# Retention and gated experts on one core: norm steps on VectorE, operand sums one chunk later, other order of the products

## The chip, the cores and the metric

The kernel runs on one core of one Trainium2 chip. A core has five engines with queues of their own: TensorE (PE in the rows; PEld is its weight load), VectorE (DVE), ScalarE (ACT), GpSimd (POOL) and SyncE (SP, which here issues most DMAs), and 16 DMA engines. The metric is the device time of one execution in microseconds (us).

## The reference

Three steps, one after the other: a retention (linear attention with a decay per head), an RMS norm with a SiLU-gated block, and four ReLU experts weighted by normalised probabilities.

```python
# B=2, H=8, S=768, D=64; gamma = 1 - 2**(-5-h), scale = 1/8
for t in range(S):
    state = gamma * state + einsum('bhd,bhe->bhde', k[:, :, t], v[:, :, t])
    y[:, :, t] = scale * einsum('bhd,bhde->bhe', q[:, :, t], state)
x = y.transpose(0, 2, 1, 3).reshape(1536, 512)
xn = x / sqrt(mean(x * x, -1) + 1e-6) * rms_g
g = xn @ w_gate                                  # 512 x 1536
x2 = (g * sigmoid(g) * (xn @ w_val)) @ w_out     # 1536 x 512
p = probs / (probs.sum(-1, keepdims=True) + 1e-9)
out = sum(p[:, e:e+1] * (relu(x2 @ w1[e]) @ w2[e]) for e in range(4))
```

## The kernel before

**Retention.** The 768 tokens of each of the two batches are cut into six chunks of 128, which makes twelve chunks in a row (i = 0 to 11; the profile's f32 matmuls of 64 to 128 columns). Inside a chunk the decay is a mask on the scores; between chunks a state per head pair is carried. For chunk i the steps are: `load` (two DMAs of up to 512 KB on SP's queue: `qk`, and `vk`, which is v and a second layout of k), `prep` (k times its decay `gk`, on GpSimd), `scores` (16 records, L727, into two PSUM banks), `masked` (L734: scores times `mask` into `am`, two VectorE products), `q_table` (L711, a matmul that spreads five small tables `gq` over partitions, copied by ACT), `prep_q` (L704: q times `gq`, on GpSimd or VectorE), `mix` (L745: `am` times v, 8 matmuls of 64 columns; L755: the state's copy `S` times q, 4 matmuls of 128 columns, added to them; then on ACT square with a row sum L765, root L767 and `vv` L769; then the state's update L781 and ACT's two copies of it, L789). A matmul of f32 shows as two records in the rows, so a chunk has 16 records of L745 and 8 of L755.

**Norm and operands.** `normal` takes the reciprocal of the root (L796, VectorE) and refines it by one Newton step in three ACT instructions (L799 to L801), with `vv`, `less` and `more` as its inputs; `normal2` (L807, VectorE) multiplies row and gain and writes `xn`. `to_x` turns `xn` by four transposes into a PSUM bank (L829) and makes from it operands of a block product in which 7 products do the work of 8. Each operand is kept as two fp32r halves, hi and lo. A chunk of a batch's first block (chunks 0 to 2 and 6 to 8) is split from the bank (hi on ACT, L839; lo on VectorE, L842) and copied for later (`first`, L845). A chunk of the second block needs sums with `first`: B22's hi (L857, ACT), two sums (L859, L861) and B22's lo (L863), all of the last three on VectorE, then two more sums and the splits of `tsum` (`split`, L815 and L818).

**Order.** In iteration i of the chunk loop TensorE does scores(i+1), mix(i), the state of i and the transposes of chunk i−1. Between the steps `pace.fill` lets waiting tasks in: conversion and sums of weights, splits, weight loads. `Pace` keeps an estimated clock for each queue (`work`, `did`, `need`), and a task goes to the engine that it reckons free first; where a task has a choice (`"PV"`), the estimate decides between GpSimd and VectorE. The order on each engine is fixed when the program is built. Buffers rotate: three for each load, two for `am`, `xn` and `tsum`, one for `first`, six PSUM banks.

**Start.** Ten zero matmuls (`warm`, L718) fill TensorE, then two matmuls (L913) spread the decays from two small inputs, `right` and `left`, then two more zeros, scores(0) and scores(1). DMAs that SP and ACT issue use eight semaphores in turn; the ninth issue waits for the landing of the first, and so on.

**After the retention** come the products of the gate, value and output matrices and of the experts (`winograd`, L523; `kept` L532 holds partial results), up to the end at 850 us.

## Time and profile before

| what | value |
| --- | --- |
| time, median of 3 (lowest to highest) | 851.85 us (851.7 to 852.69) |
| profiled execution | 851.76 us |
| its span in the trace | 850.0 us |
| TensorE busy | 835.3 us, 98% |
| VectorE, ScalarE, GpSimd busy | 543.8, 433.3, 582.0 us |
| chain that ended last | PE 86%, DVE 6%, ACT 4% |

The span is what the trace covers; the 1.76 us to the profiled execution's time lie around it. Times in the rows count from the span's start. A busy share is a mean over stages, so the stages are looked at one by one in the rows below: the stretch up to 9.3 us is the start, up to about 75 us the retention runs with weight conversion beside it, and from there on the products.

### The profile page before, as it was taken

The numbers are of one execution on the slowest core, as the hardware profiler recorded it, in microseconds if no ns is written. First come the engines' busy times: TensorE is split into PE (matmuls) and PEld (weight loads), VectorE is DVE, ScalarE is ACT, GpSimd is POOL, SyncE is SP. The second block draws the span as 40 slices with busy tenths as digits, with TensorE's granted clock in tenths as the row PEclk, the third lists the DMA queues.
The fourth block names the chain that finished last, engine by engine and source line by source line (L and its number), as shares of the span: only waits on it lengthen the run. The fifth ranks groups of instructions, "written<-read, shape, count | busy, mean of one in ns | idle before, by whom it ended". The sixth has DMA issues, their size and how long they took to land.

```text
span 850.0 us, 13945 instructions
## 1 busy us (share of the span) xinstructions
PE 835.3 (98%) x5167; PEld 795.3 (94%) x5167; DVE 543.8 (64%) x976; ACT 433.3 (51%) x971; POOL 582.0 (68%) x710
## 2 busy tenths in 40 slices
PE   8989999999999999899999999999999999999998
PEld 7879999999999999889999999999999999999987
DVE  4886867779686847842665565566466466556664
ACT  4788765445443546566444534544545454454421
POOL 3456847364454558669789888988988988988500
PEclk9999999999999999999999999999999999999999
DMA  8941232212122101100110111011011011101003
GB/s 274 308 167 51 75 100 75 75 59 91 51 74 76 49 25 27 38 25 25 50 38 27 37 38 38 26 43 33 25 51 27 25 50 38 34 30 38 1 13 136
DMA packets 29232, 52.37 MB, mean 62 GB/s; under 512 B 3988, under 2 KB 12724, under 8 KB 29164
## 3 DMA queue, kind: packets, MB, share of 16 engines
q1 hardware_dynamic: 28880, 51.24, 19.0%
q8 instruction: 40, 0.66, 0.3%
q10 hardware_dynamic: 284, 0.24, 0.1%
q14 instruction: 28, 0.23, 0.1%
HBM read 48.33 MB, written 3.15 MB: 61 GB/s over the span
## 4 chain that ended last, share of the span: by engine, by line
PE 86%; DVE 6%; ACT 4%; POOL 1%; issue 1%; DMA 1%; SPq 0%; DVEq 0%; ACTq 0%
PE bank L523 42%; PE bank L1231 7%; PE bank L1269 6%; PE bank L1270 6%; PE bank L1268 6%; PE cross L1231 5%; PE bank L1082 3%; PE bank L1083 3%; PE bank L1081 3%; PE bank L745 2%; DVE s L616 1%; POOL x2Tlo L1034 1%; PE bank L727 1%; DMA qk<-in_qk_dram 1%; DVE kept L613 1%
## 5 line engine op out<-in xcount | busy, mean ns | idle before, releaser
L532 ACT COPY kept<-bank 128x384 f32<-128x384 f32 x168 | 80.7, 481 | 122.2 <-PE bank L523 111.8
L1208 DVE SCALAR_TENSOR_TENSOR oacc<-cross,p_sb,oacc 128x256 f32<-128x256 f32 (+1 forms) x126 | 65.6, 566 | 64.2 <-PE cross L1231 64.2
L1276 DVE SCALAR_TENSOR_TENSOR oacc<-bank,p_sb,oacc 128x512 f32<-128x512 f32 (+1 forms) x97 | 72.2, 745 | 51.9 <-PE bank L1270 51.8
L1137 POOL TENSOR_TENSOR hs<-h,hs 128x384 fp32r<-128x384 f32 x97 | 97.7, 1023 | 0.7 <-ACT hs L1135 0.6
L523 PE MATMUL bank<-x2Thi,widehi 128*128 128x384 f32 x256 | 87.8, 343 | 0.7 <-DVE kept L1114 0.7
L523 PE MATMUL bank<-x2Thi,widelo 128*128 128x384 f32 x256 | 86.1, 336 | 0.0
L523 PE MATMUL bank<-x2Tlo,widehi 128*128 128x384 f32 x256 | 85.9, 336 | 0.0
L1270 PE MATMUL bank<-plainhi,hs 128*128 128x512 f32 (+1 forms) x218 | 85.1, 390 | 0.0
L1269 PE MATMUL bank<-plainlo,hs 128*128 128x512 f32 (+1 forms) x218 | 85.0, 390 | 0.0
L1268 PE MATMUL bank<-plainhi,hs 128*128 128x512 f32 (+1 forms) x218 | 84.3, 387 | 0.0
L621 POOL TENSOR_TENSOR hlo<-s,hhi 128x384 fp32r<-128x384 f32 x48 | 52.9, 1104 | 30.7 <-ACT hhi L618 24.1
L1117 ACT ACTIVATE hs<-kept 128x384 fp32r<-128x384 f32 x54 | 28.5, 527 | 86.9 <-DVE kept L1114 86.8
L1082 PE MATMUL bank<-hlo,plainhi 128*128 128x384 f32 x192 | 64.4, 335 | 1.8 <-POOL hlo L621 1.8
L523 PE MATMUL bank<-xThi,widehi 128*128 128x384 f32 x192 | 64.4, 336 | 0.0
L523 PE MATMUL bank<-xThi,widelo 128*128 128x384 f32 x192 | 64.2, 334 | 0.0
L523 PE MATMUL bank<-xTlo,widehi 128*128 128x384 f32 x192 | 64.2, 334 | 0.0
L1083 PE MATMUL bank<-hhi,plainlo 128*128 128x384 f32 x192 | 64.1, 334 | 0.0
L1081 PE MATMUL bank<-hhi,plainhi 128*128 128x384 f32 x192 | 64.1, 334 | 0.0
L1208 DVE SCALAR_TENSOR_TENSOR oacc<-bank,p_sb,oacc 128x512 f32<-128x512 f32 x84 | 59.2, 745 | 6.4 <-PE bank L1231 6.4
L464 POOL TENSOR_TENSOR downlo<-down,downhi 128x512 fp32r<-128x512 f32 x28 | 36.3, 1299 | 37.3 <-ACT downhi L460 37.3
L395 POOL TENSOR_TENSOR widelo<-sums,widehi 128x512 fp32r<-128x512 f32 x44 | 58.0, 1317 | 5.3 <-ACT widehi L390 4.9
L1143 POOL TENSOR_TENSOR h<-h 128x384 f32<-128x384 f32 x55 | 56.0, 1018 | 4.2 <-ACT h L1156 2.2
(182 smaller groups left out, 2538.8 us busy)
## 6 DMA issues: line engine op xcount, KB each, us to landing
wst<-in_moe_w_dram SPq DMA_DIRECT2D x64, 256.0 KB, 2.8
qk<-in_qk_dram SPq DMA_DIRECT2D x12, 512.0 KB, 5.7
wst<-in_moe_w_gate_dram SPq DMA_DIRECT2D x12, 512.0 KB, 3.8
wst<-in_moe_w_val_dram SPq DMA_DIRECT2D x12, 512.0 KB, 3.8
wst<-in_moe_w_out_dram SPq DMA_DIRECT2D x12, 512.0 KB, 3.8
vk<-in_vk_dram SPq DMA_DIRECT2D x10, 512.0 KB, 5.7
out_dram<-oacc SPq DMA_DIRECT2D x11, 256.0 KB, 2.0
vk<-in_vk_dram SPq DMA_DIRECT2D x2, 256.0 KB, 4.4
```

Source lines behind the costliest of these rows:

```text
L523: nc.tensor.matmul(out=ps, lhsT=lhs, rhs=rhs, start=(first and j == i == 0), stop=(j == KH - 1 and i == 2), skip_group_check=not first,)
L532: nc.scalar.copy(out=t, in_=ps)
L1081: nc.tensor.matmul(out=ps, lhsT=whi[:, c], rhs=hi, start=(f == 0), stop=False)
L1082: nc.tensor.matmul(out=ps, lhsT=whi[:, c], rhs=lo, start=False, stop=False)
L1083: nc.tensor.matmul(out=ps, lhsT=wlo[:, c], rhs=hi, start=False, stop=(f == NF - 1))
L1137: 0, "PV", TB, lambda eng: eng.tensor_tensor(out=lo, in0=t, in1=hi.bitcast(F32), op=ALU.subtract), [high]
L1208: run = lambda eng: eng.scalar_tensor_tensor(out=acc, in0=ps, scalar=pe, in1=acc, op0=ALU.mult, op1=ALU.add)
L1231: nc.tensor.matmul(out=where[c], lhsT=lhs[:, cols], rhs=rhs, start=bool(i == 0 and opens and opens(c)), stop=(i == 2), skip_group_check=True,)
L1268: nc.tensor.matmul(out=ps, lhsT=hi[:, c], rhs=whi[:, cols], start=(f == 0), stop=False)
L1269: nc.tensor.matmul(out=ps, lhsT=hi[:, c], rhs=wlo[:, cols], start=False, stop=False)
L1270: nc.tensor.matmul(out=ps, lhsT=lo[:, c], rhs=whi[:, cols], start=False, stop=(f == NF - 1))
L1276: nc.vector.scalar_tensor_tensor(out=acc, in0=ps, scalar=pe, in1=acc, op0=ALU.mult, op1=ALU.add)
```

## The change

1. **Norm's steps.** The ACT instruction for `vv` and the three of the Newton step become one `tensor_scalar` and two `scalar_tensor_tensor` on VectorE around the reciprocal (four VectorE instructions of 128x1 per chunk). `less` and `more` are gone.
2. **Operand sums later.** `to_x` is cut in two: the transposes stay, and what reads their bank (`from_x`) is kept in `taken_x` for chunks 1 to 9 and issued in the next iteration behind `normal2`.
3. **First block.** ACT copies the bank to `first`; hi and lo are split from that copy, lo on GpSimd or VectorE.
4. **Start.** `right` is loaded on SP's queue, ahead of all; seven zeros stand between scores(0) and scores(1); q_table(0) and q_table(1) come after the products of chunk 0, and q of chunk 1 is multiplied then.
5. **Products alternate.** In chunks with a state each product with `S` is issued right behind the first of its two products with `am`, so `q task` and `S end` are needed ahead of all.
6. **The planner's numbers.** A load counts 440 instead of 390 per half and 2.0 more for `vk`; a pair of products counts 0.68 (0.46 without a state).

```diff
-            end = pace.work("D", n * 390, pace.now)
+            end = pace.work("D", n * 440, pace.now) + (2.0 if nm == "vk" else 0.0)
...
+            if c:
+                pace.matmuls(0, pace.need(st[i]["q task"]), st[i]["S end"])
             for n in range(NP):
                 for j in range(2):
                     nc.tensor.matmul(
                         out=y[:, 2 * n + j, :], lhsT=am[:, j, n, :], rhs=vt[:, 2 * n + j, :],
...
-                pace.matmuls(0.4)
+                    if c and j == 0:
+                        nc.tensor.matmul(
+                            out=y[:, 2 * n:2 * n + 2, :].rearrange("p h d -> p (h d)"), lhsT=pairs(st[i]["q"])[:, n, :],
+                            rhs=st[i]["S"][:, n, :], start=False, stop=True, skip_group_check=True,
+                        )
+                pace.matmuls(0.68 if c else 0.46)
...
+            if i == 0:
+                q_table(0)
+                prep_q(1)
...
-            nc.scalar.activation(out=vv, in_=ss, func=AF.Identity, scale=-0.5 / DM, bias=less)
...
+            nc.vector.tensor_scalar(
+                out=vv, in0=ss, scalar1=-0.5 / DM, scalar2=-0.5 * EPS, op0=ALU.mult, op1=ALU.add
+            )
             nc.vector.reciprocal(out=r1, in_=r0)
-            end = pace.did("V", 1, end)
-
-            nc.scalar.activation(out=r0, in_=r1, func=AF.Square)
-            nc.scalar.activation(out=r2, in_=r0, func=AF.Identity, scale=vv, bias=more)
-            nc.scalar.activation(out=r1, in_=r1, func=AF.Copy, scale=r2)
-            end = pace.work("A", 420, end)
+            nc.vector.scalar_tensor_tensor(out=r2, in0=r1, scalar=r1, in1=vv, op0=ALU.mult, op1=ALU.mult)
+            nc.vector.scalar_tensor_tensor(out=r1, in0=r2, scalar=1.5, in1=r1, op0=ALU.add, op1=ALU.mult)
+            end = pace.did("V", 450, end)
...
             st[i].clear()
+            if 0 < i < NS - 2:
+                taken_x.append(lambda: from_x(i, ps))
+            else:
+                from_x(i, ps)
...
-                high = pace.add(1, "A", DM, lambda eng: eng.copy(out=hi, in_=ps), [pace.done(pace.now)])
-
-                low = pace.add(
-                    1, "V", DM, lambda eng: eng.tensor_tensor(out=lo, in0=ps, in1=hi.bitcast(F32), op=ALU.subtract),
-                    [high], port=False,
-                )
                 nc.scalar.copy(out=b1, in_=ps)
-                pace.did("A", DM)
...
+                split(b, first_block[b, "readers"], [pace.done(pace.did("A", DM))], hi, lo, b1, DM)
...
-        nc.scalar.dma_start(out=right, in_=c_right)
+        nc.sync.dma_start(out=right, in_=c_right)
...
+            if i == 0:
+                warm(7)
             if i + 1 < NS:
                 scores(i + 1)
-                for x in ((0, 1), (2, 3), (4,))[i] if i < 3 else ():
+                for x in ((), (2, 3), (4,))[i] if i < 3 else ():
                     q_table(x)
-                prep_q(i + 1)
+                if i:
+                    prep_q(i + 1)
                 masked(i + 1)
             if 0 < i < NS - 1:
                 normal2(i - 1)
+            while taken_x:
+                taken_x.pop()()
...
             mix(i)
+            if i == 0:
+                q_table(1)
```

TensorE's queue, from the program's start to the state of chunk 0 (`zeros` are warm, `rights,lefts` the decays, `qk` scores, `q_rows,picks` a q_table, `vk,am` products, `state` the state), before:

```order
L718 MATMUL bank<-zeros 128x128 x10
L913 MATMUL bank<-rights,lefts 128x512 x2
L718 MATMUL bank<-zeros 128x128 x2
L727 MATMUL bank<-qk 128x128 x16
L711 MATMUL bank<-q_rows,picks 128x512 x2
L745 MATMUL bank<-vk,am 128x64 x8
L781 MATMUL state<-vk 64x64 x8
```

and now:

```order
L910 MATMUL bank<-rights,lefts 128x512 x2
L718 MATMUL bank<-zeros 128x128 x2
L727 MATMUL bank<-qk 128x128 x8
L718 MATMUL bank<-zeros 128x128 x7
L727 MATMUL bank<-qk 128x128 x8
L747 MATMUL bank<-vk,am 128x64 x8
L711 MATMUL bank<-q_rows,picks 128x512
L780 MATMUL state<-vk 64x64 x8
L711 MATMUL bank<-q_rows,picks 128x512
```

The two scores stand seven zeros apart, and the two tables have moved behind the products and behind the state.

SP's queue at the start, with the semaphores of earlier DMAs (DMAHW) that an issue waits for, before:

```order
L678 DMA qk<-in_qk_dram 128x1024
L885 DMA square<-in_c_square_dram 128x128
L678 DMA vk<-in_vk_dram 128x1024
L896 DMA gk<-in_c_k_dram 128x48
L678 DMA qk<-in_qk_dram 128x1024
L678 DMA vk<-in_vk_dram 128x1024 [waits DMAHW2_49]
```

and now (DMAHW0 is `right`'s, DMAHW1 `left`'s, DMAHW2 that of the first `qk`):

```order
L879 DMA right<-in_c_right_dram 16x1024
L678 DMA qk<-in_qk_dram 128x1024
L882 DMA square<-in_c_square_dram 128x128
L678 DMA vk<-in_vk_dram 128x1024
L893 DMA gk<-in_c_k_dram 128x48 [waits DMAHW0_49]
L678 DMA qk<-in_qk_dram 128x1024 [waits DMAHW1_49]
L678 DMA vk<-in_vk_dram 128x1024 [waits DMAHW2_49]
```

`right` is issued first, and `gk` and the second `qk`, which waited for nothing, wait for a landing each.

VectorE's queue around the first chunk with sums (`r` are the norm's small steps, `am` the masked scores), before:

```order
L859 TENSOR_TENSOR tsum<-bank,first 128x256
L861 TENSOR_TENSOR tsum<-bank,tsum 128x256
L863 TENSOR_TENSOR xB22lo_89<-bank,xB22hi_88 128x2x128
L796 RECIPROCAL r_526<-r_525 128x1
L734 TENSOR_TENSOR am<-bank,mask 128x512 x2
L807 SCALAR_TENSOR_TENSOR xn<-bank,r_526,g_sb 128x512
```

and now:

```order
L795 TENSOR_SCALAR vv<-ss 128x1
L798 RECIPROCAL r_525<-r_524 128x1
L799 SCALAR_TENSOR_TENSOR r_526<-r_525,vv 128x1
L800 SCALAR_TENSOR_TENSOR r_525<-r_526,r_525 128x1
L734 TENSOR_TENSOR am<-bank,mask 128x512 x2
L806 SCALAR_TENSOR_TENSOR xn<-bank,r_525,g_sb 128x512
L857 TENSOR_TENSOR tsum<-bank,first 128x256
L859 TENSOR_TENSOR tsum<-bank,tsum 128x256
L861 TENSOR_TENSOR xB22lo_89<-bank,xB22hi_88 128x2x128
```

The three instructions that read the bank of the transposes stand behind the next `xn` instead of ahead of the norm, and the norm's other small steps stand with the reciprocal.

## Rows read from the trace of the kernel before

**Rows 1.** Busy us (instructions) of PE, PEld, DVE, ACT, POOL; clock, DMA share, GB/s

```profile
9.30:34.30 25.00, 25.00 (x275) 22.05 (x277) 17.77 (x35) 19.13 (x53) 10.41 (x9) 1.00 0.91 300
34.30:68.42 34.12, 30.79 (x356) 27.59 (x357) 27.91 (x58) 26.06 (x79) 19.23 (x20) 1.00 0.51 180
...
100.00:300.00 200.00, 199.68 (x1147) 198.23 (x1146) 148.50 (x280) 104.33 (x229) 103.32 (x129) 1.00 0.23 72
```

**Rows 2.** Timeline of TensorE, start: start us, us, instruction [idle before <- releaser]

```profile
1.05 4.63 PE L718 MATMUL bank<-zeros 128*128 128x128 f32 x20 [1.05 <-DVE zeros L890]
6.47 0.83 PE L913 MATMUL bank<-rights,lefts 128*128 128x512 f32 x2 [0.79 <-DVE lefts L909]
7.14 0.60 PE L718 MATMUL bank<-zeros 128*128 128x128 f32 x4
7.68 1.16 PE L727 MATMUL bank<-qk 64*128 64x128 f32 x16
9.30 1.16 PE L727 MATMUL bank<-qk 64*128 64x128 f32 x16 [0.46 <-DMA qk<-in_qk_dram]
```

**Rows 3.** DMA issues of 1 to 3.5 us: KB, median us to landing

```profile
qk<-in_qk_dram SPq DMA_DIRECT2D x2, 512.0 KB, 6.5
...
right<-in_c_right_dram ACTq DMA_DIRECT2D x1, 64.0 KB, 4.6
```

**Rows 4.** Timeline of the queues' DMA issues at the start

```profile
0.87 0.40 ACTq L882 DMA_DIRECT2D right<-in_c_right_dram  x1
...
2.78 0.44 SPq L678 DMA_DIRECT2D qk<-in_qk_dram  x1
```

**Rows 5.** DMA issues of the stretch 18.3 to 19 us, the same columns

```profile
qk<-in_qk_dram SPq DMA_DIRECT2D x1, 512.0 KB, 3.9
```

**Rows 6.** Waits of TensorE, 34.3 to 68.42 us: total, times, longest us

```profile
PE bank L829 <- DVE xn L807: 2.7, 4, 1.3
PE bank L727 <- DMA qk<-in_qk_dram: 0.7, 1, 0.7
```

**Rows 7.** Timeline of all queues, 34 to 42 us

```profile
34.31 0.33 SPq L315 DMA_DIRECT2D wst<-in_moe_w_out_dram  x1
...
34.73 0.38 SPq L678 DMA_DIRECT2D qk<-in_qk_dram  x1
...
41.07 1.16 PE L727 MATMUL bank<-qk 64*128 64x128 f32 x16 [0.66 <-DMA qk<-in_qk_dram]
```

**Rows 8.** Chain of waits, one chunk: start us, us, what

```profile
25.13 1.09 PE bank L727 x16
26.22 1.93 PE bank L745 x16
28.15 0.95 PE bank L755 x8
...
29.71 0.59 PE bank L829 x4
```

**Rows 9.** Timeline of VectorE and ScalarE, 36 to 40 us

```profile
36.57 0.42 DVE L859 TENSOR_TENSOR tsum<-bank,first 128x256 f32<-128x256 f32 x1 [0.83 <-ACT xB22hi L857]
...
37.70 0.15 DVE L796 RECIPROCAL r<-r 128x1 f32<-128x1 f32 x1
...
38.61 0.30 ACT L801 ACTIVATE r<-r,r 128x1 f32<-128x1 f32 x1
...
38.96 0.74 DVE L807 SCALAR_TENSOR_TENSOR xn<-bank,r,g_sb 128x512 f32<-128x512 f32 x1
```

**Rows 10.** Timeline of ScalarE and TensorE, 45 to 49 us

```profile
46.24 0.73 ACT L789 COPY S<-state 64x256 f32<-64x256 f32 x2
...
46.73 2.00 PE L745 MATMUL bank<-vk,am 128*128 128x64 f32 x16
```

**Rows 11.** Instructions by line and form, L704: ns min/median/max, starts

```profile
L704 DVE TENSOR_TENSOR qk<-qk,gq x2: 685/988/1292, 51.4 to 55.6; 128x512 f32<-128x512 f32 x2
```

**Rows 12.** Timeline of TensorE, 92 to 95 us

```profile
93.35 0.45 PE L523 MATMUL bank<-xB22hi,widehi 128*128 128x384 f32 x1 [1.37 <-ACT kept L532]
```

More of the change, by code (lines that the diff above doesn't have):

```diff
@@ L660, in tile_retention_gated_experts @@
         g_sb = ac.tile([P, DM], F32, name="g_sb")
-        eps, less, more = (ac.tile([P, 1], F32, name=nm) for nm in ("eps", "less", "more"))
+        eps = ac.tile([P, 1], F32, name="eps")
         table = ac.tile([P, 1], F32, name="table")
@@ L748, in mix @@
                     )
-                pace.matmuls(0.4)
-                if n + 1 < NP:
-                    pace.fill(0.4)
-            if c:
-                pace.matmuls(0, pace.need(st[i]["q task"]), st[i]["S end"])
-                for n in range(NP):
-                    nc.tensor.matmul(
-                        out=y[:, 2 * n:2 * n + 2, :].rearrange("p h d -> p (h d)"), lhsT=pairs(st[i]["q"])[:, n, :],
-                        rhs=st[i]["S"][:, n, :], start=False, stop=True, skip_group_check=True,
-                    )
-                pace.fill(1.15)
-                pace.matmuls(1.15)
+                    if c and j == 0:
[4 more added lines that the diff above has]
+                pace.matmuls(0.68 if c else 0.46)
+                if n + 1 < NP:
+                    pace.fill(0.68 if c else 0.46)
+            if i == 0:
+                q_table(0)
+                prep_q(1)
             xn = ap2.tile([P, DM], F32, tag="xn", name="xn")
@@ L768, in mix @@
             end = pace.did("A", 1, end)
-            nc.scalar.activation(out=vv, in_=ss, func=AF.Identity, scale=-0.5 / DM, bias=less)
-            pace.did("A", 100)
             if c + 1 < NCH:
@@ L823, in to_x @@
         def to_x(i):
-            b, c = chunks[i]
-            blk, cols = c // CPB, slice(c % CPB * P, (c % CPB + 1) * P)
             ps = pairs(bank())
@@ L831, in to_x, with from_x @@
             st[i].clear()
+            if 0 < i < NS - 2:
+                taken_x.append(lambda: from_x(i, ps))
+            else:
+                from_x(i, ps)
+        taken_x = []
+        def from_x(i, ps):
+            b, c = chunks[i]
+            blk, cols = c // CPB, slice(c % CPB * P, (c % CPB + 1) * P)
             if blk == 0:
@@ L837, in to_x @@
                 hi, lo = (x[:, :, cols] for x in xs[b]["X"])
-                where = banks.readers[-1]
-                high = pace.add(1, "A", DM, lambda eng: eng.copy(out=hi, in_=ps), [pace.done(pace.now)])
-                low = pace.add(
-                    1, "V", DM, lambda eng: eng.tensor_tensor(out=lo, in0=ps, in1=hi.bitcast(F32), op=ALU.subtract),
-                    [high], port=False,
-                )
                 nc.scalar.copy(out=b1, in_=ps)
-                pace.did("A", DM)
-                where += [high, low]
-                x_tasks[b] += [high, low]
+                split(b, first_block[b, "readers"], [pace.done(pace.did("A", DM))], hi, lo, b1, DM)
                 return
@@ L876, in to_x @@
                 split(b, readers, dep, thi[:, part], tlo[:, part], t[:, part], DM, i == NS - 1)
-        for t, value in ((eps, EPS), (less, -0.5 * EPS), (more, 1.5)):
-            nc.gpsimd.memset(t, value)
+        nc.gpsimd.memset(eps, EPS)
         nc.scalar.activation(out=table, in_=eps, func=AF.Sqrt)
-        nc.scalar.dma_start(out=right, in_=c_right)
+        nc.sync.dma_start(out=right, in_=c_right)
         nc.scalar.dma_start(out=left, in_=c_left)
```

## The prediction

> **What bounds the kernel now.** I read first the table by stretches, whose columns show how long each engine was busy. From 100 to 300 us TensorE is busy 199.68 of 200.00 us [rows 1]: there it is the bound, and nothing that the other engines save can shorten it. The change reorders work only in the retention (up to about 75 us) and in the first products that are laced into it; from about 100 us on every engine's order is row for row what it was. So what counts is how much sooner or later TensorE arrives at 100 us. In the retention it is idle 34.12 − 30.79 = 3.33 us of the stretch 34.30 to 68.42, and not at all in the one before it, which is busy 25.00 of 25.00 us [rows 1]. The granted clock is 1.00 in all three stretches, the upper of its two levels (2.4 GHz), so no term here is one of clock.
>
> Second, the timeline of TensorE's first 10 us [rows 2]: it starts at 1.05, is idle 0.79 us before L913 (for `lefts`) and 0.46 us before the second scores (for the load of `qk`). Third, the table of waits of the stretch 34.3 to 68.4 [rows 6]: four waits of L829, the transposes, for `xn`, 2.7 us in all and 1.3 at most, and one of 0.7 us of the scores for a `qk` load. Together they are the 3.33. Fourth, single rows: what a chunk costs on TensorE [rows 8], what stood ahead of `xn` on VectorE [rows 9], and one wait of 1.37 us at 93.35 [rows 12].
>
> **The change, part by part.** The sum is made on the profiled execution, 851.76 us, which is 0.09 us below the median of 851.85.
>
> *Start (T1).* Four edits meet here. The DMA of `right` goes from ACT's queue to the head of SP's, seven zero matmuls stand between the first and the second scores, and q_tables 0 and 1 move behind the products of chunk 0. The first ten zeros end at 1.05 + 4.63 = 5.68, and nothing after them can be earlier. From there I keep the old path: scores began at 7.68, 1.21 us after L913 began (6.47) [rows 2]. If L913 follows the zeros at once, scores(0) begin at 5.68 + 1.21 = 6.89 and end 1.09 later [rows 8], at 7.98. Two zeros took 7.68 − 7.14 = 0.54 us [rows 2], so seven take 1.89, and scores(1) begin at 9.87 where they began at 9.30: +0.57. That is the low end. If the zeros ran at the price of the first ten (0.463 each), they would take 3.24 and the start would be 11.22, +1.9: the high end. The two tables only change places, as many as before, and cost nothing in the sum.
>
> The zeros cover a load. The DMA semaphores are handed round in eight lanes, and a DMA on a used lane waits at the head of its queue for the landing of the one eight before it. Before, `gk` and the second `qk` were among the first eight and waited for none; the second `qk` was issued at 2.78 [rows 4] and took 6.5 us [rows 3], to 9.28, with three other loads in front of it. Now `gk` waits for `right`, the second `qk` for `left`, and all of SP's later loads stand behind them. `left` takes the place on ACT's queue that `right` had. There `right` was issued at 0.87 [rows 4] and took 4.6 us [rows 3], so by these rows `left` lands at 5.47 and the second `qk` is issued near 5.5, 2.7 us later than before. A load of the same 512 KB later in the retention, with little in front of it, took 3.9 us [rows 5]. Between 3.9 (9.4) and 6.5 (12.0) I take 4.6, nearer to the first because the loads ahead of it have had 2.7 us more: 10.1, 0.2 after the zeros' end. So **T1 = +0.8**.
>
> The Trainium skill (DMA: Bandwidth & Descriptors, Anatomy of one DMA — SWDGE (gpsimd) path) gives a DMA about 2.0 us fixed plus its bytes at 436 GB/s, fitted on GpSimd's DMAs. By an estimate from that page `right`'s 64 KB would take 2.15 us and `left`'s 16 KB less, and the lanes would be free before SP asks for them. The trace disagrees for the former, 4.6 us [rows 3]; what so short a landing would do is case D.
>
> *Norm's steps and late sums (T2).* Per chunk three ACT steps of the norm and one of its inputs (`vv`) go. In their place VectorE runs four steps of 128x1 in a row. The path before was: reciprocal on VectorE at 37.70, then ACT till 38.61 + 0.30 = 38.91, 1.2 us; `xn` began at 38.96 and took 0.74 [rows 9]. A reciprocal of 128x1 is 0.15; I take 0.2 for each step, 0.8 in all. It is not on the path, since VectorE then waits for the scores anyway. In the chunks of the second block three sums (L859, L861, L863), 0.42 each [rows 9], 1.26 in all, stood ahead of reciprocal, mask products and `xn`; now they stand behind `xn`. The longest of the four waits for `xn` is 1.3 [rows 6], so with 1.26 taken from before it none keeps more than 0.1. The `qk` wait of 0.7 stays: that load was issued at 34.73 right behind a weight load at 34.31, the scores that want it began at 41.07 [rows 7], and in the new order a weight load that waits for VectorE still stands ahead of it. Left over are 0.7 + 0.1 = 0.8, so **T2 = 0.8 − 3.3 = −2.5**, between −3.3 (all gone) and −1.0 (case C). The bank that a chunk's sums read is held one chunk longer; with six banks the next to want it are the scores two chunks on, over 5 us later by the sum of one chunk's rows [rows 8], which is the cover; without it the scores wait for the three sums, the 1.26 that was gained, which is case C's price.
>
> *First block out of SBUF.* ACT copies `first`, then the two parts are split from it. It gives ACT no more work; five of six low parts go from VectorE to GpSimd, which was busy 19.23 of 34.12 us [rows 1]. Nobody waits for them before the gate's first product, so I cost it at nothing; without that cover it is case C.
>
> The Trainium skill (GPSIMD Engine Reference, 1. Specifications) says that GpSimd shares its SBUF interfaces with VectorE and contends with VectorE's instructions that have two SBUF inputs. That speaks against this part, which turns a PSUM input into an SBUF input and moves the work to GpSimd. The row on L704 agrees: 685 ns in one case on VectorE and 1292 in the other [rows 11]. By the first price the sum stays as it is; by the second it is case C.
>
> *Alternating products (T4).* 16 records of 64 columns took 1.93 us and 8 of 128 columns 0.95 [rows 8]: 0.121 and 0.119 us each, the same for both shapes. So there is no price for changing between them in these rows, and nothing to gain: **T4 = 0**. The dearest row near is the transposes, 0.59 / 4 = 0.147 [rows 8]; if the 80 records of S products in ten chunks cost that instead of 0.119, +2.2, which only the high end could hold. What alternation does bring is a need: S and q must be ready at the start of the products, 1.9 us earlier than before (case A).
>
> *The wait at 93.35 (T3).* It is 1.37 us for ACT's `kept` [rows 12], which stands behind the last splits. GpSimd has two fewer of them late, but VectorE has two more, 0.685 each [rows 11]. Bounds −1.37 (gone) and +0.7 (one of the two in front); **T3 = −0.5**, a little over a third of it.
>
> Sum: 851.76 + 0.8 − 2.5 − 0.5 + 0 = 849.56, so **849.6**.
>
> **Rivals.**
> A, slower: the states' copies come too late. For chunk 7 S was copied from 46.24 to 46.97, while the products that now need it at once began at 46.73 [rows 10]; before they had 1.93 us more. Were S 0.4 late in each of ten chunks, it costs 4.0: 853.6. It decides from about 0.25 us per chunk. Against it: in the other chunks the copies ended 0.2 us or more before. 0.08.
> B: the second `qk` comes late. Issued at 5.5 and with its old 6.5 us it lands at 12.0, 2.7 after 9.30: T1 = +2.7 and the total 851.76 + 2.7 − 3.0 = 851.5. For it: `vk` and the square share the engines with it as before. Against: they were issued long before it now. 0.15.
> C: VectorE becomes the bound. If GpSimd slows it as L704's two prices say, mask and sums take back what the order gave: T2 = −1.0, the total 851.1. For it: VectorE was already busy 27.91 of 34.12 us [rows 1]. 0.14.
> D: transfers land after a short fixed time, T1 = +0.57: 849.3. The 4.6 us [rows 3] are against it, save that `right`'s queue is now another. 0.12.
>
> **How the numbers follow.** Forecast 0.51, A 0.08, B 0.15, C 0.14, D 0.12. The low end takes T1 +0.57, T2 −3.3, T3 −1.0: 848.0. The high end takes T1 +1.9, T2 −1.0, T3 −0.5: 852.2, which holds B and C and leaves A out. A measurement can tell 0.2% of this time, 1.7 us; faster means below 850.15, slower above 853.55. Faster: four in five of the forecast and all but little of D are 0.52; same: B, C and the rest, 0.40; slower: A, 0.08.
>
> **What would show it.** Right: scores(1) start near 10 us with at most 0.3 us idle before; no wait of L829 for `xn` over 0.3 us between 34 and 68 us; the order of products as long as before (2.9 us per chunk). Wrong: an idle time before scores(1) of over 1.5 us (B); waits of the products on `S` or `qk` (A); mask products over 0.75 us each or a wait of L829 of over 0.5 us (C); a product record over 0.13 us (T4). If TensorE's busy time after 100 us is other than before, the whole reading of what bounds it was wrong.

## The result and the profile after

The changed kernel took 860.38 us (median of 5 runs, 855.31 to 862.09), the kernel before 851.85 us (851.7 to 853.58) beside it. The ratio is 1.0072, with an interval of 1.0045 to 1.01: slower by 0.7%, where 849.6 (848.0 to 852.2) and 0.3% faster were forecast. The profiled execution is the longest of the five, 862.09 us with a span of 860.3; its mean clock was 0.99, and the times of the five fall roughly as their mean clock rises (855.31 at 0.998, 860.38 at 0.994; 861.1 at 0.996 is out of line).

The table by stretches of the changed kernel, with the columns of [rows 1]:

```profile
9.30:34.30 25.00, 24.61 (x271) 21.78 (x272) 17.99 (x38) 14.61 (x36) 13.02 (x13) 1.00 0.88 289
34.30:68.42 34.12, 28.73 (x279) 25.92 (x279) 32.71 (x64) 17.00 (x43) 20.49 (x23) 0.87 0.54 191
68.42:100.00 31.58, 30.57 (x218) 28.79 (x218) 23.89 (x46) 20.72 (x48) 24.00 (x25) 0.92 0.12 34
100.00:300.00 200.00, 199.04 (x1139) 196.91 (x1138) 149.68 (x280) 105.74 (x233) 106.11 (x133) 1.00 0.24 76
```

In the second row three things stand against [rows 1]. TensorE is idle 34.12 − 28.73 = 5.39 us instead of 3.33. VectorE is busy 32.71 of 34.12 us instead of 27.91, which leaves it hardly any time to wait in. And the clock is 0.87, and 0.92 in the next row, where it was 1.00.

The waits of TensorE from 34.3 to 76.8 us, up to the first product of the gate (total, times, longest; before: [rows 6]):

```profile
PE bank L826 <- DVE xn L806: 5.2, 4, 1.8
PE bank L752 <- DVE qk L704: 0.2, 1, 0.2
```

The waits that the late sums were to remove are longer, 5.2 us instead of 2.7, and still as many. The wait for a `qk` load (0.7) is gone. A table by stretches of 5 us shows where the clock was:

```profile
40.00:45.00 5.00, 3.54 (x28) 3.08 (x29) 4.89 (x12) 2.39 (x7) 2.16 (x3) 0.75 0.89 320
45.00:50.00 5.00, 5.00 (x59) 4.35 (x57) 4.43 (x9) 2.74 (x8) 4.26 (x4) 0.91 0.16 54
...
60.00:65.00 5.00, 3.41 (x27) 3.02 (x28) 4.93 (x12) 3.03 (x8) 1.51 (x3) 0.80 0.55 190
65.00:70.00 5.00, 5.00 (x36) 4.77 (x36) 4.47 (x9) 1.11 (x5) 2.82 (x4) 0.50 0.19 75
70.00:75.00 5.00, 5.00 (x38) 4.45 (x38) 2.49 (x7) 3.20 (x8) 1.91 (x2) 0.68 0.34 105
```

Twice TensorE stands still for part of a stretch (3.54 and 3.41 of 5.00), and twice the lower level (0.5 in the column, 1.2 GHz) begins there. Each missing tenth of a stretch of 5 us is half a microsecond of work not done, which gives an estimate: 1.25 + 0.45 + 1.0 + 2.5 + 1.6 = 6.8 us. TensorE's busy time from the second scores to the first product of the gate, the same 629 records in both kernels, bears it out, before and after:

```profile
9.30:68.42 59.12, 55.79 (x629) 49.63 (x630) 45.69 (x93) 45.20 (x132) 29.64 (x29) 1.00 0.68 231
```

```profile
9.65:76.89 67.24, 61.80 (x629) 55.25 (x630) 55.42 (x112) 36.76 (x93) 36.95 (x38) 0.90 0.62 211
```

The same work took 6.0 us more, and the idle time grew from 3.3 to 5.4 us.

What made `xn` late is seen in VectorE's small steps, by line over the whole span (ns min/median/max):

```profile
L795 DVE TENSOR_SCALAR vv<-ss x12: 139/146/154, 14.4 to 83.1; 128x1 f32<-128x1 f32 x12
L798 DVE RECIPROCAL r<-r x12: 144/154/164, 14.7 to 83.2; 128x1 f32<-128x1 f32 x12
L799 DVE SCALAR_TENSOR_TENSOR r<-r,vv x12: 219/278/1290, 14.9 to 83.4; 128x1 f32<-128x1 f32 x12
L800 DVE SCALAR_TENSOR_TENSOR r<-r,r x12: 159/160/1280, 15.2 to 83.7; 128x1 f32<-128x1 f32 x12
```

All four handle one element per partition. The two with one input tensor never pass 0.17 us; the two with two input tensors go from 0.16 up to 1.29. The timeline of all engines ahead of the longest wait:

```profile
55.76 2.67 POOL L693 TENSOR_TENSOR vk<-vk,gk 128x512 f32<-128x512 f32 x2
...
57.52 0.15 DVE L798 RECIPROCAL r<-r 128x1 f32<-128x1 f32 x1
...
57.70 0.75 DVE L799 SCALAR_TENSOR_TENSOR r<-r,vv 128x1 f32<-128x1 f32 x1
...
58.40 1.27 POOL L817 TENSOR_TENSOR xTlo<-tsum,xThi 128x512 fp32r<-128x512 f32 x1
...
58.48 1.20 DVE L800 SCALAR_TENSOR_TENSOR r<-r,r 128x1 f32<-128x1 f32 x1
...
59.60 1.27 DVE L734 TENSOR_TENSOR am<-bank,mask 128x512 f32<-128x512 f32 x2
...
60.80 0.73 DVE L806 SCALAR_TENSOR_TENSOR xn<-bank,r,g_sb 128x512 f32<-128x512 f32 x1
...
61.59 0.66 PE L826 MATMUL bank<-square,xn 128*128 128x128 f32 x4 [1.84 <-DVE xn L806]
```

L799 ends at 58.45, when GpSimd's pair ends (55.76 + 2.67 = 58.43). L800 ends at 59.68, when GpSimd's next instruction ends (58.40 + 1.27 = 59.67). Each step, which takes 0.22 (L799) or 0.16 us (L800) at the least, lasted until GpSimd was through. It is so in the whole profile: 11 of the 24 steps took more than 0.3 us, and each of the 11 ended 0.01 to 0.03 us behind a GpSimd instruction that it had run beside. The reciprocal ahead of them, with one input, ran in 0.15 beside the same GpSimd pair. Behind them on VectorE stand the mask products, `xn`, and with it TensorE.

### The profile page after: what moved, and what is told of

It is laid out like the page before. It is cut to its first block, busy times and chain, and to the rows that moved or that the text cites. A ratio compares the mean times of both kernels' runs of the same rounds, so it can differ in the third digit from the quotient of the medians.

```text
span 860.3 us, 13944 instructions
## 1 busy us (share of the span) xinstructions
PE 844.3 (98%) x5181; PEld 803.8 (93%) x5181; DVE 557.0 (65%) x1001; ACT 421.7 (49%) x923; POOL 591.8 (69%) x719
## 4 chain that ended last, share of the span: by engine, by line
PE 87%; DVE 8%; POOL 1%; issue 1%; DMA 1%; ACT 1%; DVEq 0%; ACTq 0%
PE bank L523 44%; PE bank L1235 7%; PE bank L1273 6%; PE bank L1274 6%; PE bank L1272 6%; PE cross L1235 5%; PE bank L1086 4%; PE bank L1087 4%; PE bank L1085 3%; PE bank L727 1%; PE bank L747 1%; POOL x2Tlo L1038 1%; DVE am L734 1%; DVE r L800 1%; DVE xn L806 1%
## 5 line engine op out<-in xcount | busy, mean ns | idle before, releaser
L395 POOL TENSOR_TENSOR widelo<-sums,widehi 128x512 fp32r<-128x512 f32 x48 | 63.4, 1320 | 14.1 <-ACT widehi L390 12.6
L621 POOL TENSOR_TENSOR hlo<-s,hhi 128x384 fp32r<-128x384 f32 x47 | 51.5, 1098 | 29.4 <-ACT hhi L618 24.4
```

## The experiments

Theory V: a VectorE instruction with two input tensors in SBUF waits for GpSimd's instruction to end, so the two new steps cost up to 1.29 us and not 0.2, and `xn` and TensorE are late. Theory C: TensorE's idle time then lets the clock fall. Rival R: it is the other parts (late sums, first block, alternating products), or the mere number of VectorE's instructions. Times are medians, and ratios are to the kernel before on the same chip in the same hours (medians of 851.3 to 852.2 us).

A median can move without the edit. Behind the wait of 1.6 us for GpSimd's `hlo` (L621, near 350 us), which every kernel here has, the clock fell in five of the eighteen profiles (the changed kernel, e6, g2, g3, g4), and that cost some 1.7 us. The executions of the kernel before differ in the same way: beside e6 they took 851.1 to 851.6 us at a mean clock of 0.999 or more and 852.5 to 854.1 at 0.998; where theirs fell isn't recorded. So where two kernels are close, "at full clock" below means their executions with a mean clock of 0.999 or more.

**e1: the two steps with one input tensor each.** The order on all engines stays; the second tensor becomes a scalar operand. I call it the mended kernel.

```diff
-nc.vector.scalar_tensor_tensor(out=r2, in0=r1, scalar=r1, in1=vv, op0=ALU.mult, op1=ALU.mult)
-nc.vector.scalar_tensor_tensor(out=r1, in0=r2, scalar=1.5, in1=r1, op0=ALU.add, op1=ALU.mult)
+nc.vector.tensor_scalar(out=r2, in0=r1, scalar1=r1, scalar2=vv, op0=ALU.mult, op1=ALU.mult)
+nc.vector.tensor_scalar(out=r1, in0=r2, scalar1=1.5, scalar2=r1, op0=ALU.add, op1=ALU.mult)
```

> The changed kernel, with the two norm steps L799 and L800 written as tensor_scalar: one tensor input and scalars, where they were scalar_tensor_tensor with two tensor inputs. The order of all engines stays. Theory V (a step with two SBUF inputs waits until GpSimd's instruction is over): each of the two steps stays under 0.25 us, as vv and the reciprocal between them did (0.154 and 0.164 at most), where they went up to 1.29 and 1.28; TensorE waits for xn under 2 us in all instead of 6.1, no stretch before 76 us is at half clock, and the time is 849 to 851. Rival R (VectorE has too much work, or the other parts are to blame): the waits for xn stay above 4 us and the time above 855.

Measured: 852.98 us, ratio 0.9996 (0.9977 to 1.0016). The steps, by line:

```profile
L799 DVE TENSOR_SCALAR r<-r,vv x12: 272/273/276, 15.2 to 75.3; 128x1 f32<-128x1 f32 x12
L800 DVE TENSOR_SCALAR r<-r,r x12: 214/214/216, 15.6 to 75.6; 128x1 f32<-128x1 f32 x12
```

No spread is left, though 0.27 is a little above the 0.25 expected. The waits for `xn` fell from 6.1 us in the whole span to 1.7, and the clock is 1.00 in every stretch of the profile (851.47 us); the first product of the gate starts at 67.10 instead of 76.89 (68.42 before). The median came out 2 us above what was expected: four executions at full clock took 851.3 to 851.7, six at 0.997 or 0.998 took 853.0 to 853.2. In the profile, the 1.3 us won in the retention shrink to 0.3 at the end: a wait of 0.8 for the last `xn` is new, and `kept` costs 1.3 us in four waits where it cost 1.4 in the one of [rows 12]. Theory V holds; 7 us of the loss hang on the form of two instructions.

**e2: the small steps back on ScalarE.**

```diff
-nc.vector.tensor_scalar(out=vv, in0=ss, ...)
+nc.scalar.activation(out=vv, in_=ss, func=AF.Identity, scale=-0.5 / DM, bias=less)
...
-nc.vector.scalar_tensor_tensor(out=r2, ...)
-nc.vector.scalar_tensor_tensor(out=r1, ...)
...
+nc.scalar.activation(out=r0, in_=r1, func=AF.Square)
+nc.scalar.activation(out=r2, in_=r0, func=AF.Identity, scale=vv, bias=more)
+nc.scalar.activation(out=r1, in_=r1, func=AF.Copy, scale=r2)
```

> The changed kernel with the norm's small steps back on ScalarE as they were before; the other parts of the change stay. Theory V: the waits for xn fall under 3 us and the time to 849 to 853, since the steps cannot wait for GpSimd. Rival R (late sums, first block on GpSimd or alternating products are to blame): the waits for xn stay above 4 us and the time above 855.

Measured: 852.56 us, ratio 1.0012 (1.0001 to 1.0024). The waits for `xn` are down to 0.5 us, as theory V wants. Others took their place. The timeline of TensorE:

```profile
54.04 0.49 PE L752 MATMUL bank<-S,qk 128*128 128x128 f32 x2 [1.65 <-ACT S L790]
60.62 0.49 PE L752 MATMUL bank<-S,qk 128*128 128x128 f32 x2 [1.25 <-ACT S L790]
```

This is the forecast's rival A: with the products alternating, the state's copies are needed at once, and with the small steps on its queue ScalarE makes them late, 3.1 us in three waits. In e1, where the steps are on VectorE, no wait for `S` is left.

**e3: the small steps on VectorE alone**, in the change's form, put on the kernel before (the first hunk of the change on `vv` and `normal`, nothing else).

```diff
...
-end = pace.work("A", 420, end)
+nc.vector.scalar_tensor_tensor(out=r2, in0=r1, scalar=r1, in1=vv, op0=ALU.mult, op1=ALU.mult)
+nc.vector.scalar_tensor_tensor(out=r1, in0=r2, scalar=1.5, in1=r1, op0=ALU.add, op1=ALU.mult)
+end = pace.did("V", 450, end)
```

> The kernel before with the norm's small steps on VectorE as the change writes them (scalar_tensor_tensor), and no other part. Theory V: the two steps go above 0.6 us in some chunks, the waits for xn grow from 2.7 us to 4 or more, and the time is above 853. Rival R: both steps near 0.2 us and the time within 851 to 853, or below, because ScalarE's 1.2 us chain is gone.

Measured: 859.64 us, ratio 1.0095 (1.0078 to 1.0111): by itself as slow as the whole change. Waits for `xn` 9.7 us in five, 3.4 at most. Rival R's parts (late sums, first block, alternating products) fall: none of them is in this kernel. Its other half, the mere number of VectorE's instructions, falls with e1, which has as many.

**e4: zeros in the changed kernel's waits.**

```diff
+for n in range({3: 4, 4: 5, 6: 2, 7: 6}.get(i, 0)):
+    nc.tensor.matmul(out=ps[:, 0, :], lhsT=zeros, rhs=zeros, start=True, stop=True)
 for n in range(KD):
     nc.tensor.transpose(ps[:, n, :], xn[:, n * P:(n + 1) * P], ident)
```

> The changed kernel with zero matmuls on TensorE just ahead of the transposes of chunks 3, 4, 6 and 7 (4, 5, 2 and 6 of them, 0.27 us each, into the bank of the transposes), where it waited 1.15, 1.46, 0.76 and 1.84 us for xn. xn comes as late as before. Theory C (TensorE's idle time is what lets the granted clock fall): no half clock between 42 and 46 and between 63 and 73 us, which cost some 1.7 and 5.1 us, and the time is 852 to 856. Rival (the clock falls for another reason, or the late xn itself is the loss): half clock stays, and the time is 859 to 862.

Measured: 861.21 us, ratio 1.0092 (1.0058 to 1.0126), in the rival's range, but four runs from 856.26 to 871.3. In the profiled one (856.26) the clock is 1.00 up to 100 us and the first product of the gate starts at 71.12 instead of 76.89, as theory C wants. The other three runs had mean clocks of 0.982 to 0.994, and where theirs fell isn't recorded. As a test it decides nothing, so that for the changed kernel's own waits theory C stays argued.

**e5: the steps alone, with one input tensor.** As e3, with the two lines of e1.

```diff
-nc.vector.scalar_tensor_tensor(out=r2, in0=r1, scalar=r1, in1=vv, op0=ALU.mult, op1=ALU.mult)
+nc.vector.tensor_scalar(out=r2, in0=r1, scalar1=r1, scalar2=vv, op0=ALU.mult, op1=ALU.mult)
...
```

> The kernel before with the norm's small steps on VectorE, written with one tensor input each; no other part of the change. Theory V: both steps stay under 0.3 us as in the mended kernel, so what the steps alone cost with two inputs (+7.5 us, to 859.6) is gone, and ScalarE's chain of 1.2 us with it: waits for xn at most the 2.7 us of before, time 850.5 to 852.5. Rival (any small step on VectorE is in the way of the mask products, whatever its form): waits for xn above 4 us and a time above 854.

Measured: 854.36 us (851.14 to 859.58), ratio 1.0028 (1.0005 to 1.0051), against 859.64 with two inputs. Of the waits for `xn` one is left, but it is long: 2.64 us, ending at 42.00, behind operand sums and a first block's low part on VectorE. So taking ScalarE's chain away is no gain by itself, and the expectation of 850.5 to 852.5 was too good. The half clock that follows this one wait made it the test for theory C.

**f4: eight zeros in that one wait.**

```diff
+for n in range(8 if i == 4 else 0):
+    nc.tensor.matmul(out=ps[:, 0, :], lhsT=zeros, rhs=zeros, start=True, stop=True)
```

> The kernel before with the steps on VectorE in the one-input form (854.4 us), plus eight zero matmuls (2.2 us) on TensorE ahead of the transposes where it waited 2.64 us for xn at 42.00; from 41.8 to about 52 it ran at half clock then. Theory C (the granted clock falls because TensorE had idled): xn comes as late, but no stretch between 40 and 55 is at half clock, the first product of the gate comes some 3 to 5 us sooner than 71.66, and the time is 850.5 to 852.5 with no execution above 854. Rival: half clock comes all the same and the time stays at 853.5 to 856.

The table by stretches without the zeros (e5):

```profile
40.00:45.00 5.00, 3.00 (x20) 2.50 (x20) 3.58 (x10) 1.30 (x4) 0.93 (x1) 0.64 0.84 323
45.00:50.00 5.00, 5.00 (x36) 4.74 (x35) 3.70 (x6) 1.29 (x5) 4.73 (x5) 0.50 0.00 0
50.00:55.00 5.00, 5.00 (x44) 4.54 (x42) 4.47 (x11) 1.89 (x5) 3.28 (x4) 0.83 0.32 108
```

and with them (f4):

```profile
40.00:45.00 5.00, 4.92 (x50) 4.45 (x48) 4.07 (x12) 1.98 (x5) 2.74 (x3) 1.00 0.95 368
45.00:50.00 5.00, 4.38 (x56) 3.89 (x54) 4.83 (x11) 2.80 (x8) 5.00 (x6) 1.00 0.34 117
50.00:55.00 5.00, 4.67 (x58) 4.13 (x57) 4.38 (x15) 3.56 (x10) 3.02 (x4) 1.00 0.46 160
```

The transposes came no sooner, at 42.12 instead of 42.00, since `xn` was as late; but the clock stayed at 1.00, and the first product of the gate starts at 68.52 instead of 71.66. The time is 852.46 us (850.6 to 853.27), ratio 0.9987 (0.9966 to 1.0008); no run is above 854, where six of ten were without the zeros (e5). Work that computes nothing, put where TensorE waited, won back 3.1 us at the first product and 1.9 in the medians. Theory C holds for this wait. The length of a wait does not settle it, though: four of e5's ten executions had a mean clock of 0.998 or more, and waits of 1.84 us in e7's profile and of 1.47 in e8's brought no fall, where one of 1.46 did in the changed kernel's.

**e6, e7, e8: one other part undone in the mended kernel.** The start of before:

```diff
-nc.sync.dma_start(out=right, in_=c_right)
+nc.scalar.dma_start(out=right, in_=c_right)
...
-if i == 0:
-    warm(7)
...
-for x in ((), (2, 3), (4,))[i] if i < 3 else ():
+for x in ((0, 1), (2, 3), (4,))[i] if i < 3 else ():
...
```

> The mended kernel (one input per norm step) with the start of before: right on ScalarE's queue, no seven zeros, the first two q tables behind the second scores. If the start's term (T1) was read rightly, the second scores begin at 9.2 to 9.4 instead of 9.96 and the first product of the gate (67.10) comes 0.6 sooner; the end moves by 0 to -0.6, since the products behind it wait for their weights. Rival: the zeros save more later than they cost here, and the first product comes no sooner than 67.1.

Measured: 852.17 us, 0.9994 (0.9982 to 1.0006). The second scores start at 9.01 instead of 9.96 and the first product at 66.12 instead of 67.10. The medians differ by 0.8 us and the ratios hardly; at full clock it is 849.9 to 850.9 against 851.3 to 851.7. The new start costs about 1 us and gives nothing back that these runs show.

The products apart (the loop of the products as it was before):

```diff
-                    if c and j == 0:
-                        nc.tensor.matmul(
...
+            if c:
+                pace.matmuls(0, pace.need(st[i]["q task"]), st[i]["S end"])
+                for n in range(NP):
...
```

> The mended kernel with the products with S behind those with am again, as before. If alternation is worth nothing (T4 = 0), a chunk's products take 2.88 us (2.82 when alternating), waits for S or q vanish (0.2 us), and the time is within 1 us of the mended kernel's 853.0. Rival A (early need of S and q costs): it is faster by 1 us or more.

Measured: 851.5 us, 0.9985 (0.996 to 1.0009), 1.5 below the mended kernel; the wait for `q` is gone. That is past the 1 us that was set for no difference, and at full clock it is 848.8 to 849.5 against 851.3 to 851.7. By the number rival A came, but the 0.2 us of its waits cannot be the cause; what the 2 us are is not shown. One wait for `xn`, of 1.84 us, is left in the profile, and five of the ten executions have mean clocks of 0.993 to 0.996 and take 852.4 to 853.9, which hides part of it in the median.

The operand sums at once:

```diff
-            if 0 < i < NS - 2:
-                taken_x.append(lambda: from_x(i, ps))
-            else:
-                from_x(i, ps)
+            from_x(i, ps)
```

> The mended kernel with the operand sums issued at once again, ahead of the next norm steps, mask products and xn. If they stood in the way of xn (T2), the waits for xn grow from 1.7 by 1.5 to 3 us between 34 and 68 us, the first product of the gate comes at 68.5 to 70 instead of 67.10, and the time is 853 to 856 with a chance of stretches at half clock. Rival (the small steps off ScalarE were the whole gain): waits and first product within 0.5 us of the mended kernel's.

Measured: 850.53 us, 0.9986 (0.9975 to 0.9997). As expected the waits for `xn` grew to 3.4 us and the first product came at 69.08; against the expectation the time is lower than the mended kernel's, not higher. The waits behind the retention, 1.3 us for `kept` there, are 0.2 us here. Where the retention ends does not tell where the kernel ends. The order of the conversion work behind it changes with such edits (between the kernel before and the changed one VectorE's, ScalarE's and GpSimd's orders differ until some 160 us), which fits, but was not tested apart.

**f1, f2, f3: two of these undone at once.** f1 has the edits of e6 and e7, f2 those of e7 and e8, f3 those of e6 and e8, in the mended kernel.

> The mended kernel (one input per norm step) with the start and the order of products of before; late sums and first block out of SBUF stay. If the single results add up, the second scores begin at 9.0 and the first product of the gate at about 66.9 (67.7 without the start's part, 66.1 without the products'), and the time is 849 to 851.5, below before by 0.0 to 0.3%. Rival (the time behind the retention is set by the weights' conversion): no better than either alone, 851.5 to 852.2.

> The mended kernel with the order of products and the sums of before; the new start and the first block out of SBUF stay. If late sums and alternation only cost, the time is 849 to 850.5, as good as with the sums at once (850.5) or better. Rival (late sums are worth something once the products stand apart): waits for xn above 3.4 us in all, stretches at half clock, 852 or more.

> The mended kernel with the start and the sums of before; alternating products and the first block out of SBUF stay. Without the start's 0.9 us the first product of the gate comes at about 68.2 instead of 69.08, and the time is 849.5 to 851. Rival: the products behind absorb it, the time stays at 850.5 or above.

Measured: f1 849.74 us, 0.996 (0.9938 to 0.9983); f2 852.18, 0.9998 (0.998 to 1.0016); f3 850.39, 0.9965 (0.9949 to 0.9981). f1 and f3 came as expected, f2 did not: its time is the rival's, its waits for `xn` (1.9 us) are not. With products apart the late sums are worth 0.7 us (e7 against f2) and 1.6 (f1 against g1, below); with alternating products they cost 2.4 (e1 against e8) and 1.8 (e6 against f3). Each is near what these medians can tell. At full clock the four are 2.4, 2.8, 1.4 and 1.6 us, and in none of the pairs do the two kernels' times overlap: the sign of one part hangs on the other.

**g1, g2: the first block.** g1 is f1 with the sums at once, that is, the steps alone (e5) with the first block out of SBUF and the planner's load numbers, which no run changes alone. g2 is e6 with the first block split from PSUM:

```diff
-split(b, first_block[b, "readers"], [pace.done(pace.did("A", DM))], hi, lo, b1, DM)
+high = pace.add(1, "A", DM, lambda eng: eng.copy(out=hi, in_=ps), [pace.done(pace.now)])
+low = pace.add(
+    1, "V", DM, lambda eng: eng.tensor_tensor(out=lo, in0=ps, in1=hi.bitcast(F32), op=ALU.subtract),
```

> The kernel before with the norm's steps on VectorE in the one-input form and the first block split out of SBUF (and the planner's load numbers); start, products and sums as before. It differs from the steps alone (854.4 us, one wait for xn of 2.64 us, where a first block's low part on VectorE stood ahead of the mask products) by the first block only. If that part takes work off VectorE that stood in the way: no wait for xn above 1.5 us, no half clock, 849 to 851.5. Rival (its low parts on GpSimd slow VectorE's two-input work): waits for xn as long or longer, 853 or more.

> The mended kernel with the start of before (852.2 us) and the first block's parts split from PSUM again, lo on VectorE; late sums and alternating products stay. If the first block's part takes work off VectorE: waits for xn grow from 1.7 to 3 us or more and the time to 853 or more. Rival: waits for xn within 0.5 us of 1.7 and the time 851 to 852.5, so that the part is worth nothing.

Measured: g1 851.34 us, 1.0012 (0.9992 to 1.0032), 3 below e5 and without its long wait (at full clock the two are close, 850.7 to 851.5 against 851.1 and 851.7; two of g1's ten executions have a mean clock under 0.998, six of e5's); g2 848.89, 0.9958 (0.9944 to 0.9973), 3.3 below e6, with waits for `xn` of 0.9 us. So the part pays where the sums stand ahead of `xn` (it takes a low part from there; the load numbers may have a share), and costs where they stand behind. The second expectation failed with both its branches: neither longer waits nor the same time.

**g3, g4: two parts of the change alone, and the form of the steps once more.** g3 is f1 with the edit of g2: the kernel before with two parts of the change alone, the steps in the one-input form and the late sums (and the planner's load numbers). g4 is g2 with the two lines of e1 turned back.

> The kernel before with two parts of the change alone: the norm's steps on VectorE in the one-input form, and the operand sums one chunk later (and the planner's load numbers). It differs from the run with the first block split from PSUM (848.9 us) by the order of products. If alternation is worth nothing, waits for xn stay under 1.5 us and the time is 848 to 850. Rival (alternation carries part of the 848.9): 850.5 or more.

> The fastest kernel so far (848.9 us: steps with one input, late sums, alternating products, start and first block of before) with the two steps back in the two-input form and nothing else. Theory V: both steps go above 0.7 us in some chunks, each ending with an instruction of GpSimd, the waits for xn grow from 0.9 us to 3 or more, and the time to 853 or more. Rival (with these parts there is room for them): waits under 2 us, time under 851.

Measured: g3 847.18 us (846.23 to 852.65), ratio 0.9944 (0.9922 to 0.9967): faster than the kernel before and the changed one, and below the 848 to 850 expected. Its retention in the table by stretches:

```profile
34.30:68.42 34.12, 34.12 (x380) 31.26 (x376) 32.44 (x79) 22.66 (x61) 26.44 (x30) 1.00 0.56 196
```

TensorE is busy 34.12 of 34.12 us: all 3.33 us of [rows 1] are gone, and the first product starts at 64.44 instead of 68.42.

g4: 854.31 us, 1.0025 (1.0012 to 1.0039), 5.4 above g2. Its timeline:

```profile
49.95 2.67 POOL L693 TENSOR_TENSOR vk<-vk,gk 128x512 f32<-128x512 f32 x2
...
51.89 0.75 DVE L796 SCALAR_TENSOR_TENSOR r<-r,vv 128x1 f32<-128x1 f32 x1
...
52.58 1.27 POOL L814 TENSOR_TENSOR xTlo<-tsum,xThi 128x512 fp32r<-128x512 f32 x1
...
52.67 1.20 DVE L797 SCALAR_TENSOR_TENSOR r<-r,r 128x1 f32<-128x1 f32 x1
...
55.78 0.66 PE L824 MATMUL bank<-square,xn 128*128 128x128 f32 x4 [1.84 <-DVE xn L803]
```

The steps end at 52.64 and 53.87, GpSimd's instructions at 52.62 and 53.85. So the two-input form decides the sign in g2's order too. That the waits for `xn` grow to 2.9 us and not to the 3 or more expected is at the edge; the half clock (0.85 from 34.30 to 68.42) adds to them.

## Why the prediction was wrong

**What bounds the kernel** held: TensorE is the bound (busy 199.04 of 200.00 us from 100 to 300 us, 199.68 before), and the change decides in the retention. But "no term here is one of clock" did not. It rested on the clock of before, 1.00, and left out that the change itself could make TensorE wait longer than it had, with a fall of the clock behind the waits.

**T1, the start: +0.8 forecast, +0.35 in this pair of profiles and about +0.9 over all.** The second scores start at 9.65 instead of 9.30. The DMA issues and the timelines at the start, after:

```profile
right<-in_c_right_dram SPq DMA_DIRECT2D x1, 64.0 KB, 2.1
...
left<-in_c_left_dram ACTq DMA_DIRECT2D x1, 16.0 KB, 3.2
```

```profile
4.08 0.33 SPq L678 DMA_DIRECT2D qk<-in_qk_dram  x1
```

```profile
7.33 1.83 PE L718 MATMUL bank<-zeros 128*128 128x128 f32 x14
9.65 1.16 PE L727 MATMUL bank<-qk 64*128 64x128 f32 x16 [0.50 <-DMA qk<-in_qk_dram]
```

The lanes work as described: the second `qk` is issued at 4.08, when `left` landed (0.87 + 3.2). But the landing was sooner than forecast (4.07 against 5.47) and the load slower: 9.65 − 4.08 = 5.6 us where 4.6 was taken. The 2.1 us of `right` are what the Trainium skill's estimate gives (DMA: Bandwidth & Descriptors, Anatomy of one DMA — SWDGE (gpsimd) path: 2.15 for 64 KB, fitted on GpSimd's DMAs), whereas `left`, a quarter of that, took 3.2. The 4.6 of [rows 3] was not the price of 64 KB alone: `right` took 2.0 to 2.1 us in the seven profiles with the new start and 4.0 to 4.7 in the eleven with the old one; what held it on ACT's queue is not shown. The seven zeros cost as forecast (1.83 against 1.89), and scores(0) ran earlier, by 7.68 − 6.24 = 1.4 us. The ten zeros still stand ahead of the decays (1.05, 4.34 us), though the listing of TensorE's queue after the change begins behind them.

One pair of profiles says little here. The second scores start at 9.65 to 10.31 us in the seven profiles with the new start (median 9.93) and at 8.70 to 9.60 in the eleven with the old one (median 9.04). So the size of T1 was right, by an earlier issue and a slower load than those it was summed from.

**T2, the retention: −2.5 forecast, about +8.1 measured.** This is the step that failed. From the second scores (+0.35) to the first product of the gate (76.89 − 68.42 = +8.47) the kernel lost 8.12 us. The idle time within it grew by 2.1: 5.2 − 2.7 = 2.5 for `xn` and 0.2 for `q`, less the 0.7 of the `qk` wait that went. The other 6.0 are TensorE's longer busy time for the same records: the half clock, 6.8 by the estimate above, and the alternating products, −0.6 (below). That the waits let the clock fall is argued from e5 and f4, not shown in this kernel. Two things were mis-sized. First, "I take 0.2 for each step": the price came from the reciprocal of [rows 9], which has one input tensor, and was put on two instructions with two. Their own mean between 34 and 68 us was 0.51 and 0.63. The cover named for them, VectorE's wait for the scores, was 0.5 us in that stretch, and the kernel before had shown none there. [rows 11] held the right price: the same VectorE instruction at 685 and at 1292 ns. In the trace of the kernel before, a GpSimd instruction ran beside the slow one and none beside the quick one:

```profile
51.43 0.69 DVE L704 TENSOR_TENSOR qk<-qk,gq 128x512 f32<-128x512 f32 x1
...
55.28 1.04 POOL L693 TENSOR_TENSOR vk<-vk,gk 128x512 f32<-128x512 f32 x1 [4.67 <-DMA vk<-in_vk_dram]
55.58 1.29 DVE L704 TENSOR_TENSOR qk<-qk,gq 128x512 f32<-128x512 f32 x1
```

I weighed it, with the Trainium skill's sentence (GPSIMD Engine Reference, 1. Specifications), against the first block's low parts, and not against the new small steps, which have two SBUF inputs as well. The trace shows these steps, of one element per partition, waiting out what GpSimd has left to do. Second, the half clock, of which there was no term.

**Case C** named the port and the engine, at 0.14, and priced it at T2 = −1.0; its sign to tell, a wait of L829 above 0.5 us, came. It had the neighbour right, but not the small steps as its victims, and put 1.5 us more than the forecast into T2 where 10.6 came. Of the victims that it named, the mask products and the three sums that read the bank have one SBUF tensor and were not slowed: the mask products took 680 ns (682 before), the first of the sums 411 (425). The two further sums of a chunk, of two SBUF tensors, were slowed: on VectorE they took 0.42 us before and 1.12 to 1.49 in the changed kernel (L865 and L869, three instructions). e1 still has such rows (1.26 and 1.48), so they are not the loss that e1 takes away.

**Late sums** did what was forecast once the steps were mended: with products, start and first block as before (g3) the wait for `xn` is gone altogether. Their worth for the whole time hangs on the order of the products (f1 to f3).

**T4, alternation: 0 forecast.** A chunk's products took 2.82 us (31.78 to 34.60) instead of 2.88, −0.06 a chunk. Case A did not come in the changed kernel (0.2 us for `q`), but did as soon as ScalarE kept the norm's steps (e2, 3.1 us in three waits). For the whole time alternation is not worth nothing: at full clock it costs 2.0 us (e1 against e7), 2.5 (e6 against f1) and 0.8 (g2 against g3) with late sums, and gains 1.7 (e8 against f2) and 1.9 (f3 against g1) with the sums at once. By which waits is not shown.

**T3, the wait at 93.35: −0.5 forecast.** From the gate's first product to the product that waited there, the changed kernel won 8.47 − 7.61 = 0.9 us: the wait of 1.37 is gone, one of 0.9 for the last `xn` is new. It lost more behind, in a place the forecast did not look at: by the product at 395.63 before (405.95 after) it was 10.3 us behind, 2.7 more than at that product. Of these, 1.7 are a stretch at clock 0.83:

```profile
350.00:360.00 10.00, 8.24 (x37) 7.61 (x37) 5.91 (x10) 4.09 (x9) 9.76 (x9) 0.83 0.01 2
```

Two waits for `kept`, 0.27 and 0.51, make most of the rest. The fall of the clock is no work of the change: it is the one of five of the eighteen profiles. "From about 100 us on every engine's order is row for row what it was" holds for TensorE alone; VectorE's, ScalarE's and GpSimd's orders differ until some 160 us.

Left open: why TensorE's clock falls behind the wait of 1.6 us for L621 in some executions and not in others; how the half clock was spread over the four unprofiled runs; and what the planner's numbers do by themselves, which no run changed alone.

## What to carry to other kernels

Before work is moved to VectorE, count the input tensors of each instruction and look for GpSimd beside it: a step of one element per partition can last as long as GpSimd's instruction, and the same arithmetic with a scalar operand in the second tensor's place does not. On an engine that feeds the bound one in order, price such steps by their worst row, not their median. And where the bound is TensorE, a wait costs more than its length if the clock falls with it: a short look at the clock by 5 us tells which waits matter, and zeros put into the wait show what the clock alone is worth.

## What the runs showed of the hardware

In the changed kernel 13 of the 24 VectorE `scalar_tensor_tensor` of 128x1 with two SBUF inputs took 0.16 or 0.22 us; the other 11 took 0.33 to 1.29 and ended 0.01 to 0.03 us behind a GpSimd instruction. `tensor_scalar` of the same size with two scalar operands took 0.272 to 0.276 and 0.214 to 0.216 us in all twelve chunks (e1). This agrees with the Trainium skill (GPSIMD Engine Reference, 1. Specifications), which names the contention there but no size. A wait of 2.64 us of TensorE was followed by about 10 us at half clock (e5's profile), which eight zero matmuls in the wait prevented (f4's).
